# Moving each triangular inversion next to the chain that uses it, in a delta-rule and two-layer MoE kernel

## The chip, the cores and the metric

The kernel runs on one core of a Trainium2 chip. The metric is the device time of one execution in microseconds. Three runs of the kernel before took 5598.62, 1131.16 and 1135.46 us, so the median is 1135.46. The engines are named as the profile names them: PE does matmuls (PEld loads their weights), DVE, ACT and POOL do elementwise work, SP issues DMAs.

## The reference

Three stages follow each other: a delta-rule attention over 768 steps for 4 batches of 8 heads of 48 features, and two feed-forward layers of 384 to 2048 to 384 on the 3072 resulting tokens.

```
k_n = k / (norm(k) + 1e-6)
for t in range(S):                                   # state: D x D for each batch and head
    y[t]  = q[t] @ state
    v_old = k_n[t] @ state
    state = state + beta[t] * outer(k_n[t], v[t] - v_old)
x = y as 3072 tokens of 384
h = x @ w_in1;  g = where(h > 0, h, exp(min(h, 0)) - 1);  x = g @ w_out1
h = x @ w_in2;  P = a0 + a1 h + a2 h^2 + a3 h^3;  Q = 1 + |b0||h| + |b1| h^2
out = (P / (Q + 1e-6)) @ w_out2
```

All of it is float32. The kernel takes the weights as raw 64-bit words and converts them itself.

## The kernel before, in words

**Windows.** The 768 steps are cut into 12 chunks of 64 steps. Two chunks (512 tokens of the feed-forward layers) make a window; there are six, 0 to 5. While the first layer works on the tokens of window w, the attention of window w + 1 is computed beside it. Before window 0 lies a startup, and after window 5 the second layer (phase 2).

**What a window of the first layer does.** It has 16 steps f. Each f has nine large matmuls H (lines 578 to 580, two parts of each operand, so three products), the activation A1 on ACT (lines 607 to 609), B1 on DVE (line 613), C1 (gh on ACT, line 619; gl on DVE, line 621), and nine large matmuls O (lines 596 to 598). PSUM has two places for H, and gh, gl, e and pe have two buffers each. At the start of a window `split_x` makes xh (ACT, line 396) and xl (DVE, line 397) from the attention's output; at its end `evac1` (line 634) moves the layer's output out, one third of it by way of the tile `tmp`.

**What the attention of a window needs.** First the g groups (`g_item`, eight a window): eight matmuls each (line 279) of loaded keys and queries, evacuated on DVE (line 282) and ACT (lines 286 to 288) into gd, p and lo. Then the inversion (`t_pieces`): a transposition of gd (line 297), a run of tiny DVE and ACT steps (lines 301 to 333, with a large product at 324), 23 pairs of a product (line 345, always into `tmp`) and a sum (line 346) which invert 32 triangular matrices a partition (seven pairs of 8 rows, eight of 16, then four large pairs into xx_t and four into the remaining corner of tt), and a last transposition into tp_t (line 372). The tiles am, tt, tmp and tp_t exist once. Then the chain, for each of the two chunks: prep (kv on POOL, line 422; lb on ACT; four tb on POOL, line 432, out of tp_t), ks (line 449) with R on DVE (line 452), u1 (line 460) with its copies on ACT (line 463), lo (line 471) with its subtraction on DVE (line 475), u2 (line 483) with ub on ACT, the outputs y (lines 498 and 505), xx, and ku with the update of the state s_bd (line 535).

**Conversions.** 128 halves of weight tiles are loaded as raw words, treated on ACT (lines 160 and 162), then on DVE (line 179 for the first layer's 64; 176 and 177 for the second's), on ACT (180) and POOL (182), and split on ACT (71) and POOL (72).

**What sets the order.** Every step is entered in a list with a number for its place (`at(t, fn)`; one f is 1, a window 16). The list is sorted by it, and between the first steps and phase 2 a scheduler takes the numbers as priorities: it puts each engine's instructions into a fixed order, in which an instruction that it thinks isn't ready yet is passed by others. On the chip each engine runs its own order strictly. In the kernel before, window w works on the inversion of window w + 2 (numbers T + 0.6 to T + 9, where T = 16 w) and, from T + 0.6 to T + 14, on the chain of window w + 1.

Of the kernel before, what the change touches and what calls it, by code (L numbers as in the profile page):

```python
# [19 lines left out]
NF = 16  # L20
# [6 lines left out]
HD = DM // 2  # L27
NV = 15
Q = dict(
    ma=-200, xo=2.244, pg0=0, pg1=2, ca=0, g1=-72.135, g1d=1.259, t1a=-33.632, t1b=-8, npre=3, c0=-47,  # L30
    c0d=4.533, c1=-1.042, c1r=4.439, b1=0.704, c1o=0.919, h0=1.013, h0d=0.5, h1=0.586, h1d=0.462, g2=-7.824,
    g2d=1.116, g3w1=-0.578, g3=-0.806, t2=2.578, t2b=14.166, t3b=9, p=14.315, tm=4, chd=1.061, ws=0.808,
    sx=-0.529, ev=16.5, c5=1.1, c5d=0.4, l5=1.3, wu0=0, wl0=2, wd0=5, wy0=2, wm0=2, wu1=6, wl1=7, wd1=6, wy1=0,
    wm1=6, wk=4, wr=3, wr0=4)
# [3 lines left out]
def kernel(  # L38
# [19 lines left out]
    NW = len(WINS)  # L58
# [209 lines left out]
    def g_item(j, s, b):  # L268
        u0 = 16 * j + 4 * b
        if b == 0:  # L270
            p_d[s] = ap2.tile([128, 16, 64], F32, tag="p", name="p", bufs=4)
            lo_d[s] = ap2.tile([128, 8, 32], F32, tag="lo", name="lo", bufs=4)
        p_t, lo_t = p_d[s], lo_d[s]
        v0 = 4 * b
        ps = pa.tile([128, 4, 128], F32, tag="pa", name="gp")
        for p2 in range(2):
            t, n = gin_t.pop((s, b, p2))
            for i in range(2):
                mm(out=ps[:, 2 * p2 + i], lhsT=t[:, i, 0:128], rhs=t[:, i, 128:256], start=True, stop=True)  # L279
            gin_l[0] -= n  # L280
            gin_ahead(1)
        nc.vector.tensor_tensor(
            out=p_t[:, v0:v0 + 4], in0=ps[:, :, 64:128],
            in1=mp_sb[b // 2].unsqueeze(1).to_broadcast([128, 4, 64]), op=ALU.mult)
        b0, b1 = halves(b // 2)
        act(out=gd[b0, u0:u0 + 4], in_=ps[b0, :, 0:32], func=AF.Copy)
        act(out=gd[b1, u0:u0 + 4], in_=ps[b1, :, 32:64], func=AF.Copy)
        act(out=lo_t[b0, v0 % 8:v0 % 8 + 4], in_=ps[b0, :, 32:64], func=AF.Copy)
# [270 lines left out]
    def g_list(w):  # L559
        return [(lambda j=j, s=s, b=b: g_item(j, s, b)) for j, s in enumerate(WINS[w]) for b in range(4)]  # L560
# [21 lines left out]
    def H(key, f, x, NC):  # L582
        i = hn[0] % (2 if h_c is None else 3)
        hn[0] += 1
        ps = h_c if i == 2 else h_a[:, i]
        hp[key, f] = ps
        h_mms(ps[:, 0:NC], f, x, NC)

    def O(key, f, hi, lo, NC):
        gh, gl = gt.pop((key, f))  # L590
        if f == 0:
            acc[key] = [po.tile([128, 512], F32, tag=f"o{i}", name=f"o{i}") for i in range(3)]
        for c in range(3):
            ps = acc[key][c]
            cs = slice(128 * c, 128 * c + 128)
            mm(out=ps[:, 0:NC], lhsT=hi[:, cs], rhs=gh[:, 0:NC], start=(f == 0), stop=False)  # L596
            mm(out=ps[:, 0:NC], lhsT=hi[:, cs], rhs=gl[:, 0:NC], start=False, stop=False)  # L597
            mm(out=ps[:, 0:NC], lhsT=lo[:, cs], rhs=gh[:, 0:NC], start=False, stop=(f == NF - 1))  # L598
# [157 lines left out]
    def at(t, fn, *a):  # L756
        ev.append((t, len(ev), fn, a))

    def spread(t0, t1, fns, cost=None):
        cost = cost or [1.0] * len(fns)  # L760
        c = 0.0
        for fn, d in zip(fns, cost):
            at(t0 + (t1 - t0) * c / sum(cost), fn)
            c += d
# [33 lines left out]
    def t_at(w, t0, t1, t2, t3):  # L798
        tp = t_pieces(w)
        at(t0, tp[0])  # L800
        at(t0 + .3, tp[1])
        el = [4 * k * k for k in range(1, 8)] + [16 * k for k in range(8, 16)] + [1024, 768, 512, 256] + [256, 512, 768, 1024]
        spread(t1, t2, tp[2:-1], [.4 + .0021 * n for n in el])
        at(t3, tp[-1])

    def conv_at(t, d):
        at(t, conv_x)
        at(t + d, conv_d)
        at(t + 2 * d, conv_s)
# [9 lines left out]
    at(-55, load_beta, 1)  # L819
    for sl, fn in chain(0, [[0, 0, 1, 3, 5, 7, 10, 8, 11, 9], SLOTS[1]]):  # L820
        at(-48 + Q["chd"] * sl, fn)
    t_at(1, max(-47.5, Q["g1"] + 7 * Q["g1d"] + .01), Q["t1a"], Q["t1b"], Q["t1b"] + .1)
    for i in range(2 * Q["npre"]):
        conv_at(Q["c0"] + Q["c0d"] * i, 2)
    for i in range(4 * NF - 2 * Q["npre"]):
        conv_at(Q["c1"] + i / Q["c1r"], .24)

    for w in range(NW):
        T = 16 * w
        NC = 256 * len(WINS[w])  # L830
        at(T + Q["sx"], split_x, w)
        for f in range(NF):
            at(T + f, lambda w=w, f=f, NC=NC: H(w, f, xt[w], NC))
            at(T + f + .05, A1, w, f, NC)
            at(T + f + Q["b1"], B1, w, f, NC)
            at(T + f + Q["c1o"], C1, w, f, NC)
            at(T + f + Q["ws"], wo_split, w, f)

            def o1(w=w, f=f, NC=NC):
                t = oring.pop((w, f))  # L840
                O(w, f, t[:, 0], t[:, 1], NC)
            at(T + (f + 2.4 if f < NF - 2 else f + 1.95 if f == NF - 2 else f + 1.4), o1)
        at(T + Q["ev"], evac1, w)
        if w + 1 < NW:
            c0, cd = (Q["h0"], Q["h0d"]) if w == 0 else (Q["h1"], Q["h1d"])
            for sl, fn in chain(w + 1):
                at(T + c0 + cd * sl, fn)
        if w + 2 < NW:
            at(T - .2, load_beta, w + 2)
            for i, fn in enumerate(g_list(w + 2)):  # L850
                at(T + (Q["g2"] + Q["g2d"] * i if i < 4 else (Q["g3w1"] if w == 1 else Q["g3"]) * (8 - i)), fn)
            if w == 0:
                t_at(2, Q["t2"], Q["t2"] + .5, Q["t2b"], Q["t2b"] + .1)
            else:
                t_at(w + 2, T + .6, T + 1.2, T + Q["t3b"], T + Q["t3b"] + .1)
        if 1 <= w <= 4:
            for f in range(8):
                conv_at(T + 2 * f + .15, .5)

    T = 16 * (NW - 1)  # L860
# [12 lines left out]
    for k in range(NP * NG2):  # L873
        t = P + 2 * k
        at(t, H2, k)
        if k == NK - 1:
            for i in range(2):
                n = slice(512 * i, 512 * i + 512)
# [117 lines left out]
```

## Time and profile before

| | us |
|---|---|
| median of three runs | 1135.46 |
| the profiled execution | 1129.3 |
| its span | 1127.5 |
| PE busy | 1037.9 |
| DVE busy | 904.5 |
| ACT busy | 771.7 |
| POOL busy | 466.4 |

The span begins with the first instruction and ends with the last. Busy time of PE counts overlapping matmuls once and contains their pipeline, so a PE that is busy isn't at its peak; the granted clock (PEclk, 1.00 is 2.4 GHz, 0.50 is 1.2 GHz) has to be read beside it. A stretch of the run is read by the busy time of each engine in it, and the waits and the chain of waits tell which engine the others stood behind. B1 (line 613) runs once for each f, so its starts show how fast the loop goes.

### The profile page before, as it was taken

The page shows a single profiled execution, that of the slowest core. Times are in us where ns is not written, and L with a number is a line of the kernel's source. Part 1 is how long each engine was busy: PE and PEld are TensorE (multiplying, and loading weights), DVE is VectorE, ACT ScalarE, POOL GpSimd, SP SyncE. Part 2 cuts the span into 40 slices and gives each one's busy share as a digit, 9 for nine tenths or more (in the row PEclk, how much of TensorE's full clock was granted, in tenths as well). Part 3 has the DMA queues.
Part 4 walks back from the last instruction along what each step waited for, and adds up shares of the span by engine and source line. Part 5 has one row for each costly group of instructions (what it writes and reads, how often), then busy time and mean ns, then how long its engine had stood idle before and what let it go on. Part 6 is the DMA issues. An engine that isn't in the chain of part 4 may idle for free.

```text
span 1127.5 us, 20636 instructions
## 1 busy us (share of the span) xinstructions
PE 1037.9 (92%) x7952; PEld 835.8 (74%) x7952; DVE 904.5 (80%) x1240; ACT 771.7 (68%) x1525; POOL 466.4 (41%) x399
## 2 busy tenths in 40 slices
PE   7178898889798999899999999999999999999997
PEld 7155676667676778777888878778788888888885
DVE  4989889689857873795434379999999999999997
ACT  5568687866577546665665689976767667676764
POOL 1376655434332322242332145446363544536342
PEclk8559899999899989998999999999999999999999
DMA  9436343454364113120212044400100001010000
GB/s 287 155 102 200 116 147 114 131 161 126 97 189 149 59 50 121 60 81 1 81 49 62 1 148 133 120 28 1 56 1 25 32 1 56 1 56 1 29 1 28
DMA packets 51842, 91.75 MB, mean 81 GB/s; under 512 B 7072, under 2 KB 29728, under 8 KB 51744
## 3 DMA queue, kind: packets, MB, share of 16 engines
q1 hardware_dynamic: 51744, 90.43, 25.8%
q8 instruction: 62, 1.02, 0.4%
q14 instruction: 36, 0.29, 0.1%
HBM read 77.83 MB, written 12.58 MB: 80 GB/s over the span
## 4 chain that ended last, share of the span: by engine, by line
PE 54%; DVE 24%; ACT 7%; issue 6%; DMA 5%; POOL 3%; SPq 0%; ACTq 0%; DVEq 0%; POOLq 0%
PE o L733 13%; PE h_a L578 6%; PE h_a L579 6%; PE h_a L580 6%; DVE tmp L345 5%; PE o L596 3%; PE o L597 3%; PE o L598 3%; PE h_b L578 2%; PE h_b L579 2%; PE h_b L580 2%; DMA raw<-w_out 2%; DVE tt L346 2%; PE gp L279 2%; DVE wo L695 2%
## 5 line engine op out<-in xcount | busy, mean ns | idle before, releaser
L710 POOL TENSOR_TENSOR gl<-wo 128x1024 fp32r<-128x1024 f32 x47 | 147.3, 3134 | 202.4 <-DVE wo L709 174.2
L72 POOL TENSOR_TENSOR wor<-wo,wor 128x384 fp32r<-128x384 f32 x96 | 109.1, 1137 | 268.0 <-ACT wor L71 260.3
L578 PE MATMUL h_a<-xh,wi 128*128 128x512 f32 x417 | 173.9, 417 | 10.1 <-ACT pe L608 8.8
L579 PE MATMUL h_a<-xl,wi 128*128 128x512 f32 x417 | 168.9, 405 | 3.7 <-DVE xl L397 3.7
L580 PE MATMUL h_a<-xh,wi 128*128 128x512 f32 x417 | 167.8, 402 | 0.0
L733 PE MATMUL o<-gh,wo 128*128 128x512 f32 x564 | 135.9, 390 | 0.4 <-ACT ys L741 0.4
L613 DVE SCALAR_TENSOR_TENSOR e<-e,pe 128x512 f32<-128x512 f32 x96 | 70.8, 737 | 75.4 <-ACT e L609 75.1
L733 PEld LDWEIGHTS o<-gh,wo 128*128 128x128 f32 x564 | 105.2, 188 | 23.8 <-ACT ys L741 2.4
L596 PE MATMUL o<-gh,wor 128*128 128x512 f32 x288 | 115.8, 410 | 0.0
L597 PE MATMUL o<-gl,wor 128*128 128x512 f32 x288 | 114.5, 398 | 1.2 <-DVE gl L621 1.2
L598 PE MATMUL o<-gh,wor 128*128 128x512 f32 x288 | 113.0, 392 | 0.0
L578 PEld LDWEIGHTS h_a<-xh,wi 128*128 128x128 f32 x417 | 80.8, 194 | 30.5 <-ACT pe L608 10.9
L621 DVE TENSOR_TENSOR gl<-e,gh 128x512 fp32r<-128x512 f32 x88 | 79.2, 900 | 29.3 <-ACT gh L619 28.9
L579 PEld LDWEIGHTS h_a<-xl,wi 128*128 128x128 f32 x417 | 81.3, 195 | 22.1 <-DVE xl L397 7.2
L607 ACT ACTIVATE e<-h_a 128x512 f32<-128x512 f32 x91 | 54.2, 596 | 58.6 <-PE h_a L580 58.2
L580 PEld LDWEIGHTS h_a<-xh,wi 128*128 128x128 f32 x417 | 81.1, 194 | 17.3
L696 ACT ACTIVATE wo<-wo 128x1024 f32<-128x1024 f32 (+1 forms) x49 | 51.3, 1046 | 60.4 <-DVE wo L695 60.4
L619 ACT ACTIVATE gh<-e 128x512 fp32r<-128x512 f32 x96 | 60.0, 625 | 35.0 <-DVE e L613 35.0
L695 DVE SCALAR_TENSOR_TENSOR wo<-wo 128x1024 f32<-128x1024 f32 (+1 forms) x49 | 73.1, 1492 | 4.5 <-ACT wo L688 4.4
L71 ACT ACTIVATE wor<-wo 128x384 fp32r<-128x384 f32 x96 | 50.4, 525 | 35.7 <-PE o L598 35.3
L733 PE MATMUL o<-gl,wo 128*128 128x512 f32 x282 | 71.7, 389 | 0.8 <-POOL gl L710 0.8
L707 DVE SCALAR_TENSOR_TENSOR gh<-wo,ab_sb 128x1024 fp32r<-128x1024 f32 (+1 forms) x49 | 65.5, 1336 | 6.6 <-ACT wo L697 0.6
(168 smaller groups left out, 2462.8 us busy)
## 6 DMA issues: line engine op xcount, KB each, us to landing
kv<-c_kv SPq DMA_DIRECT2D x24, 576.0 KB, 4.6
gin<-g_in SPq DMA_DIRECT2D x69, 192.0 KB, 2.9
kq<-c_kq SPq DMA_DIRECT2D x22, 512.0 KB, 3.8
raw<-w_out SPq DMA_DIRECT2D x42, 192.0 KB, 2.5
raw<-w_in SPq DMA_DIRECT2D x34, 192.0 KB, 2.4
wo<-w_in SPq DMA_DIRECT2D x30, 192.0 KB, 2.7
xr<-x2d SPq DMA_DIRECT2D x6, 768.0 KB, 5.3
out_t<-ys SPq DMA_DIRECT2D x18, 256.0 KB, 2.2
```

Of the source, the lines that this page charges most:

```text
L72: eng.tensor_tensor(out=t[:, 1], in0=src, in1=t[:, 0].bitcast(F32), op=ALU.subtract)
L578: mm(out=ps, lhsT=hi, rhs=xh[:, c, 0:NC], start=(c == 0), stop=False)
L579: mm(out=ps, lhsT=hi, rhs=xl[:, c, 0:NC], start=False, stop=False)
L580: mm(out=ps, lhsT=lo, rhs=xh[:, c, 0:NC], start=False, stop=(c == 2))
L596: mm(out=ps[:, 0:NC], lhsT=hi[:, cs], rhs=gh[:, 0:NC], start=(f == 0), stop=False)
L597: mm(out=ps[:, 0:NC], lhsT=hi[:, cs], rhs=gl[:, 0:NC], start=False, stop=False)
L598: mm(out=ps[:, 0:NC], lhsT=lo[:, cs], rhs=gh[:, 0:NC], start=False, stop=(f == NF - 1))
L613: nc.vector.scalar_tensor_tensor(out=e, in0=e, scalar=-1.0, in1=p, op0=ALU.add, op1=ALU.add)
L621: eng.tensor_tensor(out=gl[:, 0:NC], in0=e, in1=gh[:, 0:NC].bitcast(F32), op=ALU.subtract)
L695: v.scalar_tensor_tensor(out=sq, in0=sq, scalar=1.0 + 1e-6, in1=ab, op0=ALU.add, op1=ALU.add)
L710: (v if k == NK - 1 else nc.gpsimd).tensor_tensor(out=gl, in0=sq, in1=ab, op=ALU.mult)
L733: mm(out=ps, lhsT=wo2[2 * j + i][:, int(p == 1), cs], rhs=(gl if p == 2 else gh)[:, n], start=(j == 0 and p == 0 and i == 0), stop=(j == N ...
```

## The change

Six inversions, their g groups and their chains are given other numbers; nothing is computed differently. From window 1 on, the g groups of window w + 1 stand at T - 11.6 to T - 6, its inversion at T - 5 to T + 4.1 (in window 0: -10 to 4.1), and its chain at T + 4.3 to T + 16. So the inversion for a chain now runs in the second half of the window before and the first quarter of the chain's own window, where before it ran one window earlier. The inversion of window 1 leaves the startup's numbers. 24 conversions instead of 6 have early numbers (-47 on, 1.9 apart instead of 4.533), and the others come 3.6 instead of 4.439 to one f.

```diff
-    ma=-200, xo=2.244, pg0=0, pg1=2, ca=0, g1=-72.135, g1d=1.259, t1a=-33.632, t1b=-8, npre=3, c0=-47,
-    c0d=4.533, c1=-1.042, c1r=4.439, b1=0.704, c1o=0.919, h0=1.013, h0d=0.5, h1=0.586, h1d=0.462, g2=-7.824,
+    ma=-200, xo=2.244, pg0=0, pg1=2, ca=0, g1=-72.135, g1d=1.259, t1a=-33.632, t1b=-8, npre=24, ta=-5, tb=4, hd=0.4, c0=-47,
+    c0d=1.9, c1=-1.042, c1r=3.6, b1=0.704, c1o=0.919, h0=1.013, h0d=0.5, h1=0.586, h1d=0.462, g2=-7.824,
...
-    t_at(1, max(-47.5, Q["g1"] + 7 * Q["g1d"] + .01), Q["t1a"], Q["t1b"], Q["t1b"] + .1)
-    for i in range(2 * Q["npre"]):
-        conv_at(Q["c0"] + Q["c0d"] * i, 2)
-    for i in range(4 * NF - 2 * Q["npre"]):
-        conv_at(Q["c1"] + i / Q["c1r"], .24)
+    for i in range(4 * NF):
+        n = Q["npre"]
+        conv_at(Q["c0"] + Q["c0d"] * i if i < n else Q["c1"] + (i - n) / Q["c1r"], 1 if i < n else .24)
...
         if w + 1 < NW:
-            c0, cd = (Q["h0"], Q["h0d"]) if w == 0 else (Q["h1"], Q["h1d"])
+            if w > 0:
+                at(T + Q["ta"] - 2, load_beta, w + 1)
+                for i, fn in enumerate(g_list(w + 1)):
+                    at(T + Q["ta"] - .2 + Q["g3"] * (8 - i), fn)
+            ta = Q["ta"] * (1 if w else 2)
+            t_at(w + 1, T + ta, T + ta + .6, T + Q["tb"], T + Q["tb"] + .1)
             for sl, fn in chain(w + 1):
-                at(T + c0 + cd * sl, fn)
-        if w + 2 < NW:
-            at(T - .2, load_beta, w + 2)
-            for i, fn in enumerate(g_list(w + 2)):
-                at(T + (Q["g2"] + Q["g2d"] * i if i < 4 else (Q["g3w1"] if w == 1 else Q["g3"]) * (8 - i)), fn)
-            if w == 0:
-                t_at(2, Q["t2"], Q["t2"] + .5, Q["t2b"], Q["t2b"] + .1)
-            else:
-                t_at(w + 2, T + .6, T + 1.2, T + Q["t3b"], T + Q["t3b"] + .1)
+                at(T + Q["tb"] + .3 + Q["hd"] * sl, fn)
```

What becomes of it in the engines' orders is shown at three places.

On DVE, where window 3 begins, before the change: xl is the split of the new window's input, L297 to L324 the start of window 5's inversion.

```order
L613 SCALAR_TENSOR_TENSOR e<-e,pe 128x512
L297 STREAM_TRANSPOSE am<-gd 128x1024
L397 TENSOR_TENSOR xl<-xs,xh 128x512 x3
L621 TENSOR_TENSOR gl<-e,gh 128x512
L301 TENSOR_SCALAR x<-am 128x32
...
L323 TENSOR_SCALAR nb<-x 128x32
L331 STREAM_TRANSPOSE bt<-x 128x32
L324 TENSOR_TENSOR am<-am,nb 128x1024
L613 SCALAR_TENSOR_TENSOR e<-e,pe 128x512
```

And the same place in the change:

```order
L613 SCALAR_TENSOR_TENSOR e<-e,pe 128x512
L535 TENSOR_TENSOR s_bd<-s_bd,ku 48x8x48 x2
L621 TENSOR_TENSOR gl<-e,gh 128x512
L535 TENSOR_TENSOR s_bd<-s_bd,ku 48x8x48 x2
L613 SCALAR_TENSOR_TENSOR e<-e,pe 128x512
L397 TENSOR_TENSOR xl<-xs,xh 128x512 x3
L621 TENSOR_TENSOR gl<-e,gh 128x512
L613 SCALAR_TENSOR_TENSOR e<-e,pe 128x512
```

The start of an inversion has left this place, and the chain's last updates of the state (L535) have come up to it.

On DVE at f = 10 to 11 of window 2 no inversion was under way before the change; in the change the start of the one for window 4 stands there, between two B1, with one of the chain's R (L452) in its midst:

```order
L318 TENSOR_SCALAR t_4653<-t_4653 128x32
L319 RECIPROCAL rr<-t_4653 128x32
L452 TENSOR_TENSOR R<-kv,ks 128x384
L320 TENSOR_TENSOR x<-rr 128x32
...
L324 TENSOR_TENSOR am<-am,nb 128x1024
L333 TENSOR_SCALAR bm<-bt,mh_sb 128x32 x2
L345 TENSOR_TENSOR tmp<-tt,am 128x4
L346 TENSOR_REDUCE tt<-tmp 128x4
...
L613 SCALAR_TENSOR_TENSOR e<-e,pe 128x512
```

17 of the 23 pairs follow from here to f = 14, and the last six stand at f = 2 to 5 of the next window.

On PE in window 2, at the first chunk of window 3's chain, before the change: ks and u1 (L460) stand next to each other, ahead of H.

```order
L580 MATMUL h_a<-xh,wi_628 128x512
L449 MATMUL ks<-s_bd,kq 32x48 x64
L460 MATMUL cb<-R,tb 64x48 x16
L578 MATMUL h_a<-xh,wi_792 128x512
L579 MATMUL h_a<-xl,wi_792 128x512
```

And in the change, of which the nine H and the nine O are cut to their ends:

```order
L449 MATMUL ks<-s_bd,kq 32x48 x64
L578 MATMUL h_a<-xh,wi_941 128x512
...
L580 MATMUL h_a<-xh,wi_941 128x512
L279 MATMUL gp<-gin 128x128 x4
L596 MATMUL o_3889<-gh,wor 128x512
...
L598 MATMUL o_3891<-gh,wor 128x512
L460 MATMUL cb<-R,tb 64x48 x16
```

Now 18 large matmuls and a g group stand between ks and u1.

## Rows read from the trace of the kernel before

**Rows 1.** Stretches: length, busy us of engines (count), granted clock, DMA share, GB/s.

```profile
0.00:117.30 117.30, 75.23 (x750) 56.98 (x751) 94.17 (x198) 73.32 (x237) 57.11 (x80) 0.74 0.60 183
117.30:244.50 127.20, 113.51 (x1119) 90.32 (x1119) 104.95 (x194) 96.81 (x264) 64.40 (x78) 0.96 0.45 135
244.50:363.50 119.00, 106.17 (x1076) 84.25 (x1075) 91.89 (x174) 80.09 (x198) 42.38 (x39) 0.96 0.46 136
363.50:472.20 108.70, 103.13 (x1070) 83.55 (x1070) 72.57 (x125) 64.85 (x140) 30.07 (x31) 0.95 0.24 77
472.20:567.10 94.90, 90.93 (x996) 73.47 (x996) 63.15 (x102) 56.17 (x111) 31.64 (x28) 0.96 0.17 54
567.10:655.10 88.00, 87.76 (x942) 71.15 (x941) 34.51 (x48) 56.05 (x111) 22.96 (x22) 1.00 0.11 36
...
737.00:1127.50 390.50, 382.72 (x1679) 313.59 (x1677) 370.68 (x291) 265.72 (x272) 178.84 (x79) 1.00 0.07 22
```

**Rows 2.** Chain of waits, phase 2: start, us, what.

```profile
814.02 4.08 PE o L733 x18
```

**Rows 3.** Chain of waits, where window 3 begins.

```profile
461.20 0.69 DVE e L613
461.90 1.91 DVE am L297
...
463.83 3.52 DVE xl L397 x3
...
472.17 0.70 DVE e L613
...
475.81 0.47 DVE R L452
```

**Rows 4.** Timeline of DVE into window 4: start, us, instruction.

```profile
560.95 0.69 DVE L613 SCALAR_TENSOR_TENSOR e<-e,pe 128x512 f32<-128x512 f32 x1 [1.45 <-ACT e L609]
...
567.07 0.69 DVE L613 SCALAR_TENSOR_TENSOR e<-e,pe 128x512 f32<-128x512 f32 x1 [2.20 <-ACT e L609]
```

**Rows 5.** Waits of PE in windows 2 and 3: us in total, times, longest.

```profile
PE cb L460 <- DVE R L452: 8.1, 8, 2.4
```

**Rows 6.** Stretches: the two halves of window 1.

```profile
244.50:299.80 55.30, 49.03 (x661) 39.00 (x659) 54.30 (x99) 33.09 (x76) 22.26 (x19) 0.97 0.35 105
299.80:363.50 63.70, 57.14 (x416) 45.25 (x417) 37.59 (x77) 47.00 (x122) 20.12 (x20) 0.95 0.55 163
```

**Rows 7.** Groups of instructions: busy us, mean ns of one, idle before.

```profile
L345 DVE TENSOR_TENSOR tmp<-tt,am 128x144 f32<-128x144 f32 (+17 forms) x114 | 57.5, 504 | 2.1
...
L346 DVE TENSOR_REDUCE tt<-tmp 128x4 f32<-128x4 f32 (+18 forms) x114 | 45.9, 403 | 2.6
...
L345 DVE TENSOR_TENSOR tmp<-xx_t,tt 128x256 f32<-128x256 f32 (+3 forms) x24 | 35.2, 1465 | 0.3
...
L346 DVE TENSOR_REDUCE xx_t<-tmp 128x64 f32<-128x1024 f32 (+3 forms) x24 | 19.5, 814 | 0.4
```

**Rows 8.** Stretch of the startup, line 179 alone.

```profile
0.00:117.30 117.30, 16.79 (x34) 0.74 0.60 183
```

**Rows 9.** Chain of waits in the startup.

```profile
62.74 3.58 POOL tb L432 x4
...
82.65 4.37 DMA wo<-w_in
```

**Rows 10.** Stretch of window 2, line 279 alone.

```profile
363.50:472.20 108.70, 9.25 (x64) 9.00 (x64) 0.95 0.24 77
```

**Rows 11.** Stretches of four f: windows 2 and 3.

```profile
413.80:441.00 27.20, 27.20 (x248) 22.72 (x247) 8.49 (x15) 18.94 (x44) 7.09 (x8) 0.88 0.20 64
519.50:544.30 24.80, 24.65 (x226) 19.95 (x225) 7.43 (x12) 15.72 (x32) 7.66 (x8) 0.86 0.07 22
```

**Rows 12.** Timeline of the startup, DVE and POOL.

```profile
56.56 1.96 DVE L345 TENSOR_TENSOR tmp<-xx_t,tt 128x1024 f32<-128x1024 f32 x1
...
56.79 2.18 POOL L72 TENSOR_TENSOR wi<-ce,wi 128x192 fp32r<-128x192 f32 x1 [0.47 <-ACT wi L71]
```

## The prediction, made before the changed kernel ran

> **What bounds the kernel now.** The sum is made against the profiled execution: 1129.3 us, of which 1127.5 are the span. I read the stretches first [rows 1], cut where the first B1 of each window starts (B1 is the DVE's one step per f, line 613, so its starts are a clock of the loop). The reader is to see three things there. From 737 us on PE is busy 382.72 of 390.50 at a granted clock of 1.00, in pieces of 18 matmuls that take 4.08 us [rows 2], 0.227 us each; nothing of the change is there. Window 5 (655 to 737) has neither chain nor inversion, and the change leaves it alone. So it acts on the first 655 us: a startup of 117.3 us and windows 0 to 4 of 127.2, 119.0, 108.7, 94.9 and 88.0 us, together 537.8.
>
> The windows differ by what runs beside the same 288 large matmuls (288 x 0.227 = 65.3 us). Window 4 has a chain, no inversion, no g groups, no conversions: PE is busy 87.76 of 88.00 at clock 1.00, so 88 is the price of a quiet window. Window 3 adds one inversion (DVE 63.15 us, not 34.51) and costs 7 more. Window 2 adds the eight g groups too: 108.7. Window 1 adds 27 conversions: 119.0. The clock tells of stalls: 0.95 or 0.96 in windows 0 to 3, so a tenth of the time was at the lower level and some 5% of a window, 4 to 5 us, was lost to it.
>
> Second I read the chain of waits where a window begins [rows 3]: between two B1 (461.20 and 472.17, 11.0 us) it holds DVE almost alone: the inversion's transposition, 1.91, xl, 3.52, then a row of tiny steps up to L324. Into window 4, where no inversion starts, the same two B1 are 6.1 us apart [rows 4]. So the start of an inversion costs 4.9 us at a boundary. Third, the waits in windows 2 and 3: u1 (L460) waits 8.1 us for R of the DVE [rows 5], 4 a window, because ks and u1 stand next to each other on PE there. Last, window 1 by halves [rows 6]: in the first, DVE is busy 54.30 of 55.30 us: inversion and conversions share it, and DVE decides; in the second it is busy 37.59 of 63.70.
>
> **The change part by part.** Counted in the orders, nothing is added or removed; it is moved. In startup there are 40 instead of 45 of the product-and-sum pairs of L345/L346, in window 0 23 instead of 24, in windows 1 to 3 23 as before, in window 4 six instead of none. So the load of a window hardly changes; the place in the window does: an inversion starts at f = 10, runs 17 pairs beside the second chunk of the chain before, and does its last six pairs and the final transposition in f = 2 to 5 of the next window, right ahead of the chain that needs them.
>
> *Startup.* Five pairs leave, four of them large. A large sum takes 0.814 [rows 7], its product about as much: 4 x 1.63 and a small pair of some 0.8 are 7.3 us. Four more conversions come in (38 ahead of the first B1, 34 before) at 16.79 / 34 = 0.49 us of DVE each [rows 8]: 2.0. DVE is relieved of 5 us. It was busy 94.17 of 117.30 us, but the first chain also hangs on POOL (tb, 3.58) and a load of 4.37 [rows 9]. I take -4; bounds -7 (the conversions hidden) and +2 (no gain, and the four conversions delay a step).
>
> *Window 0.* Its g groups fall from 14 to 8, and one transposition at either end of an inversion leaves. What a g group costs is bounded by two rows: eight are busy 9.25 us, overlapped by others [rows 10], and four f with four of them took 27.20 us against 24.80 without, at nearly one clock [rows 11], so 4.8 for eight. I take 7 for eight, near the middle, hence up to 5 for six. No engine alone bounds this window (PE busy 113.51, DVE 104.95, ACT 96.81 of 127.20), and the large pairs that startup loses now run in it. -3; bounds -10, +5.
>
> *Window 1.* 17 pairs and the start of the inversion move from the half that DVE fills into the half where it has 26 us free. The pairs of an inversion are (57.5 + 35.2 + 45.9 + 19.5) / 6 = 26.4 us [rows 7], with two transpositions of 1.9 some 30. The last six pairs, four products of 35.2 / 24 = 1.47 with sums of 0.814 and two smaller pairs of about 1 each, are with the last transposition 13 of that. The first half keeps the 13 us and is then PE's: half a quiet window, 44, and half the g groups, 4, are 48, and 55.30 - 48 = 7. -7; bounds -12 (the boundary's 4.9 besides) and 0 (the second half grows by as much).
>
> *Window 2.* The boundary's 4.9 us goes. The 4 us of waits for R go too: now 18 large matmuls, 4.08 us, stand between ks and u1, against two R of DVE at 0.5 [rows 3]. What comes in its place I bound from the same rows. At f = 10 to 11 the transposition (1.91), what stood between xl and B1 at the boundary (467.35 to 472.17, 4.8 [rows 3]) and both R stand between two B1: 8 us of DVE where PE has one f and ks, 5, so the B1 is 3 late, and on ACT the copies of u1's result (L463) stand behind gh of that f (L619), which waits for this B1; lo on PE waits for the copies. I take 1.5 (nothing, if two buffers cover it; 4, if they cover none). At f = 2 to 5 DVE has 13 us of inversion and four f of B1 and gl, 0.7 each, 18.6 in all, where PE has 16.3: the last transposition comes some 3 us late, and u1 of the first chunk stands behind it by way of tb on POOL. I take 3; bounds 0 and 5. -4.9 - 4 + 4.5 = -4.4, rounded to -4; bounds -9 and +5. For the clock I change nothing: stalls go and stalls come.
>
> *Window 3.* It gets eight g groups it didn't have, in a window where PE is busy 90.93 of 94.90: +7. R's waits -4, the two new waits +4.5. +8; bounds +1, +15.
>
> *Window 4.* The last six pairs fall on a DVE that is busy 34.51 of 88.00, so they cost nothing themselves; but u1 waits for their end: +3; bounds 0, +8 (with the clock's 4).
>
> *Queues.* With an inversion go one load of beta and POOL's memsets of tt, with a g group its two loads on SP; window 3 gets sixteen of them. The DMA engines are busy 0.17 of the time there, POOL 31.64 of 94.90 us [rows 1]; I count them at nothing. Loads that collide would show as g waiting for gin, on PE.
>
> Sum: -4 - 3 - 7 - 4 + 8 + 3 = -7, so 1122 for a profiled execution. The two ordinary runs shown (1131.16 and the median, 1135.46) lie 2 and 6 above the profiled one; with 4 for that, **1126 us**. A measurement of this kernel can tell about 2%, 23 us, from no change, so this is a gain on paper that most likely reads as no change.
>
> **A rule to weigh.** A product of the inversion ran on DVE from 56.56 to 58.52; a split of a conversion on POOL started at 56.79 and took 2.18: it ended 0.45 after DVE let go [rows 12]. The Trainium skill, SBUF — State Buffer, "Who interferes with whom", says that a DVE instruction with two inputs in SBUF and a GpSimd instruction that reads SBUF shut each other out for the whole instruction, by order of issue. By that, the trace agrees. In the sum a conversion on POOL costs DVE nothing; what it costs if it comes first is the fourth rival.
>
> **The rivals.** *The inversion ends too late for its chain* (slower than before). Place: the last transposition, then tb, then u1, with every large matmul queued behind u1 on PE. For it: DVE has no room at f = 2 to 5 by my own count, and tt, am and tmp exist once. Against it: the four tb take only 3.58 us, and PE has an f, ks and g groups to do meanwhile. It decides from 2 us a window in windows 1 to 4: 4 x 2 = 8 eats the gain. With 5 more in each (one f of DVE late, and the clock's loss), -7 + 20 = +13: 1129 + 13 + 4 = 1146. Chance 0.18.
>
> *The stalls go and none comes* (faster by over 2%). If both new waits are covered, windows 2 and 3 cost 88 + 7 + 2, window 4 stays 88, window 1 104, window 0 119, startup -7: 505 against 537.8 is -33, with startup -40: 1093. For it: the DVE loads are spread, and PE has chunk or g work wherever DVE has pairs. Against it: the start of an inversion is as serial at f = 10 as at a boundary. Two thirds of the way, 1104, still counts. Chance 0.20.
>
> *The change does not do what it says.* Counts by window are the same but for six pairs and six g groups, and only four conversions move ahead of the first B1. If placing by readiness evens out the rest, the time is 1129 + 4 = 1133. Chance 0.08.
>
> *POOL first.* Four more conversions, two POOL instructions each, ahead of DVE's products beside the first chain. Priced by the split that was held up, 0.45 us once it ran [rows 12], they hold DVE for up to 8 x 0.45 = 3.6 us, which takes the startup's 4: 1130. Chance 0.08.
>
> **How the numbers follow.** The forecast has 0.46, the rivals 0.18, 0.20, 0.08 and 0.08. Faster by over 2% (below 1112): most of the second rival and a tail of the forecast, 0.23. Slower by over 2% (above 1158): the end of the first rival and a little beyond it, 0.09. The rest, 0.68, is within 2%. The range goes from two thirds of the way to the second rival to a little above the first: 1105 to 1150. Within it the forecast's own cases take 1114 to 1138.
>
> **What would show it.** Window 3 longer by about 8 and window 4 by about 3, windows 1 and 2 shorter: right, step by step. B1 to B1 at the start of windows 2 and 3 near 6 us, not 11. The wait of u1 for R gone from the list, one of u1 for tb or of lo for L463 in it. The first B1 near 113. I am wrong if window 3 isn't longer (g is cheaper than I took it), if u1's waits reach 5 us in windows 1 to 4, or if the startup hasn't moved: then the first chain never hung on DVE.

## The result and the profile after

The changed kernel takes **1123.61 us** (median of six runs, 1122.40 to 1126.08), beside 1135.38 for the kernel before: a ratio of 0.9911, 95% interval 0.9883 to 0.9939. Timed again on another occasion it took 1121.45 beside 1137.35, 0.9866 (0.9811 to 0.9920). So it is faster by 1%, less than the 2% that were called a difference. Its profiled execution took 1126.08 us (span 1124.2), the longest of its six; a second profile of it, from the second occasion, has a span of 1119.8.

Stretches of the changed kernel, cut as those of before [rows 1] where each window's first B1 starts: start and end, length, busy us (count) of PE, PEld, DVE, ACT and POOL, granted clock, DMA share, GB/s.

```profile
0.00:124.20 124.20, 84.11 (x871) 61.24 (x872) 88.77 (x188) 73.08 (x234) 58.27 (x84) 0.68 0.56 172
124.20:235.70 111.50, 100.25 (x928) 77.07 (x927) 90.80 (x178) 91.87 (x247) 54.79 (x67) 0.97 0.45 135
235.70:347.10 111.40, 103.04 (x1072) 82.62 (x1071) 82.68 (x161) 77.45 (x189) 40.13 (x38) 0.95 0.45 137
347.10:452.40 105.30, 100.59 (x1071) 81.49 (x1070) 71.16 (x124) 64.59 (x141) 29.70 (x30) 0.97 0.25 81
452.40:557.40 105.00, 100.75 (x1069) 81.44 (x1068) 72.05 (x123) 64.47 (x141) 29.50 (x30) 0.97 0.24 78
557.40:651.80 94.40, 89.45 (x942) 71.75 (x941) 47.84 (x61) 55.85 (x111) 28.86 (x26) 0.96 0.10 33
```

Beside the forecast, in us ("after" is the profile above, "after, again" the second profile of the same kernel, "best" the best variant found below):

| stretch | before | forecast | after | after, again | best |
|---|---|---|---|---|---|
| startup | 117.3 | -4 | 124.2 (+6.9) | 117.8 (+0.5) | 118.8 |
| window 0 | 127.2 | -3 | 111.5 (-15.7) | 111.8 | 114.3 |
| window 1 | 119.0 | -7 | 111.4 (-7.6) | 112.0 | 110.2 |
| window 2 | 108.7 | -4 | 105.3 (-3.4) | 104.5 | 100.1 |
| window 3 | 94.9 | +8 | 105.0 (+10.1) | 107.1 | 100.2 |
| window 4 | 88.0 | +3 | 94.4 (+6.4) | 95.1 | 89.6 |
| behind | 472.4 | 0 | 472.4 | 471.5 | 471.2 |

The boundary into window 3 in the changed kernel, timeline of DVE: start, us, instruction, idle time before it.

```profile
445.25 0.88 DVE L613 SCALAR_TENSOR_TENSOR e<-e,pe 128x512 f32<-128x512 f32 x1
446.05 1.88 DVE L397 TENSOR_TENSOR xl<-xs,xh 128x512 fp32r<-128x512 f32 x3
...
452.35 0.69 DVE L613 SCALAR_TENSOR_TENSOR e<-e,pe 128x512 f32<-128x512 f32 x1 [3.00 <-ACT e L609]
```

B1 to B1 it is 7.1 us, not 11.0 [rows 3]: the transposition and the tiny steps are gone from between them, and DVE is idle for 3.00. Window 1 by halves, cut at the B1 of f = 8 as in [rows 6]:

```profile
235.70:288.70 53.00, 48.09 (x493) 38.43 (x492) 36.20 (x57) 36.52 (x89) 20.72 (x21) 0.94 0.41 125
288.70:347.10 58.40, 54.95 (x581) 44.19 (x580) 46.48 (x105) 40.93 (x101) 19.41 (x17) 0.97 0.49 148
```

DVE's 54.30 and 37.59 have become 36.20 and 46.48: the work went where there was room. Yet the half that DVE filled is only 2.3 us shorter, and the other half 5.3. The g groups have moved as well. Their matmuls (line 279: length, busy us and count of PE and PEld) in the two halves, before and after:

```profile
244.50:299.80 55.30, 1.05 (x8) 1.05 (x8) 0.97 0.35 105
299.80:363.50 63.70, 9.03 (x56) 7.91 (x56) 0.95 0.55 163
```

```profile
235.70:288.70 53.00, 7.14 (x42) 6.21 (x43) 0.94 0.41 125
288.70:347.10 58.40, 3.88 (x24) 3.42 (x22) 0.97 0.49 148
```

So four of the seven groups of the second half are now in the first. That they took up there what DVE's relief gave is likely, but no run shows it by itself.

The waits of PE in windows 2 and 3 (in total, times, longest), where [rows 5] had 8.1 us for R:

```profile
PE cb L460 <- POOL tb L432: 6.6, 4, 2.0
PE cb L471 <- ACT R L463: 2.4, 4, 1.2
```

Both waits that the prediction named have come, and R's has gone. The larger one over windows 1 to 4, and in window 4 alone:

```profile
PE cb L460 <- POOL tb L432: 14.3, 8, 3.5
```

```profile
PE cb L460 <- POOL tb L432: 5.0, 2, 3.5
```

How it arises is seen at the start of window 2, in the timelines of DVE, POOL and PE:

```profile
365.74 1.21 DVE L346 TENSOR_REDUCE tt<-tmp 128x64 f32<-128x1024 f32 x1
366.86 0.68 DVE L613 SCALAR_TENSOR_TENSOR e<-e,pe 128x512 f32<-128x512 f32 x1
367.46 2.10 DVE L372 STREAM_TRANSPOSE tp_t<-tt 128x1024 f32<-128x1024 f32 x1
...
369.64 3.93 POOL L432 TENSOR_TENSOR tb<-tp_t,bm 128x256 f32<-128x256 f32 x4 [1.23 <-DVE tp_t L372]
...
369.58 0.39 PE L598 MATMUL o<-gh,wor 128*128 128x512 f32 x1
371.74 0.31 PE L460 MATMUL cb<-R,tb 64*64 64x48 f32 x2 [1.77 <-POOL tb L432]
373.62 1.09 PE L460 MATMUL cb<-R,tb 64*64 64x48 f32 x16 [1.58 <-POOL tb L432]
```

DVE ends the last transposition at 369.56; POOL needs 3.93 us for the four tb; PE has done its large matmuls at 369.97 and waits twice in u1, 1.77 and 1.58 us, with all later work queued behind it.

### The profile page after: what moved, and what is told of

Its sections match the earlier page's. It is cut to its first block, busy times and chain, and to the rows that moved or that the text cites. A ratio compares the mean times of both kernels' runs of the same rounds, so it can differ in the third digit from the quotient of the medians.

```text
span 1124.2 us, 20682 instructions
## 1 busy us (share of the span) xinstructions
PE 1039.3 (92%) x7952; PEld 831.9 (74%) x7952; DVE 896.4 (80%) x1240; ACT 772.1 (69%) x1525; POOL 459.2 (41%) x399
## 4 chain that ended last, share of the span: by engine, by line
PE 63%; DVE 15%; ACT 8%; issue 5%; DMA 4%; POOL 4%; SPq 0%; ACTq 0%; DVEq 0%; POOLq 0%
PE o L733 13%; PE h_a L578 6%; PE h_a L579 6%; PE h_a L580 6%; PE o L596 4%; PE o L597 4%; PE o L598 4%; PE gp L279 3%; PE h_b L578 2%; PE h_b L579 2%; PE h_b L580 2%; DVE tmp L345 2%; DMA raw<-w_out 2%; DVE wo L695 2%; POOL tb L432 2%
## 5 line engine op out<-in xcount | busy, mean ns | idle before, releaser
L578 PE MATMUL h_a<-xh,wi 128*128 128x512 f32 x417 | 172.4, 414 | 3.8 <-ACT pe L608 3.0
L580 PE MATMUL h_a<-xh,wi 128*128 128x512 f32 x417 | 165.7, 397 | 0.0
L613 DVE SCALAR_TENSOR_TENSOR e<-e,pe 128x512 f32<-128x512 f32 x96 | 73.4, 764 | 53.9 <-ACT e L609 52.7
L621 DVE TENSOR_TENSOR gl<-e,gh 128x512 fp32r<-128x512 f32 x88 | 75.5, 858 | 34.2 <-ACT gh L619 33.8
L597 PEld LDWEIGHTS o<-gl,wor 128*128 128x128 f32 x288 | 55.0, 191 | 16.3 <-DVE gl L621 5.8
```

Of the source, the lines that this page charges most:

```text
L578: mm(out=ps, lhsT=hi, rhs=xh[:, c, 0:NC], start=(c == 0), stop=False)
L580: mm(out=ps, lhsT=lo, rhs=xh[:, c, 0:NC], start=False, stop=(c == 2))
L613: nc.vector.scalar_tensor_tensor(out=e, in0=e, scalar=-1.0, in1=p, op0=ALU.add, op1=ALU.add)
L621: eng.tensor_tensor(out=gl[:, 0:NC], in0=e, in1=gh[:, 0:NC].bitcast(F32), op=ALU.subtract)
```

## Experiments: u1 behind the last transposition

**tb3.** The inversion ends one f earlier, the chain stays.

```diff
-npre=24, ta=-5, tb=4,
+npre=24, ta=-5, tb=3,
-                at(T + Q["tb"] + .3 + Q["hd"] * sl, fn)
+                at(T + 4.3 + .4 * sl, fn)
```

> Edit: each inversion ends one f earlier (at f = 3, not 4, from the same start), the chain stays where it is. Theory C (end of the inversion): u1 of the first group waits for tb because the last transposition is late; the waits of u1 for tb (6.6 us in windows 2 and 3 together) shrink to under 2, windows 1 to 3 are 2 to 4 us shorter each, the whole 6 to 12 shorter (about 1114). Theory D (DVE is full): what DVE does one f earlier it takes from B1 of that f; the waits move to h_a or to lo, windows 1 to 3 change by less than 1.5 each, the whole by less than 4.

Measured 1112.37 us, 0.9787 of before (0.9727 to 0.9848). Windows 2, 3 and 4: 101.1, 100.3, 91.9; the waits for tb in windows 2 and 3 fell to 1.4 us. Theory C, though window 1, which it had 2 to 4 shorter, stayed (111.7), and window 0 got 4 longer (115.6).

**late.** The other way round: the chain moves, the inversions stay.

```diff
-                at(T + Q["tb"] + .3 + Q["hd"] * sl, fn)
+                at(T + 5.3 + .36 * sl, fn)
```

> Edit: the chain of each window starts one f later (5.3, not 4.3) with its steps 0.36 f apart instead of 0.40, so that it ends where it did; the inversions stay where they are. Theory C: the waits of u1 for tb shrink to under 2 us in windows 2 and 3 and nothing else changes: 6 to 12 us shorter (about 1114). Theory D: u1 still waits, since tb is late by more than one f (DVE and POOL in order), or the steps of the chain, now nearer to each other, wait for each other (lo for the copies of u1, u2 for lo) as much as was gained: the whole within 4 us of the changed kernel.

Measured 1109.32 us, 0.9766 (0.9717 to 0.9815). Stretches of windows 2 to 4 of this run:

```profile
346.10:446.20 100.10, 98.07 (x1073) 79.67 (x1072) 71.00 (x124) 64.55 (x141) 30.91 (x30) 1.00 0.26 86
446.20:545.60 99.40, 97.18 (x1069) 78.96 (x1068) 70.01 (x123) 64.34 (x141) 30.80 (x30) 1.00 0.26 82
545.60:636.10 90.50, 87.65 (x942) 69.91 (x941) 46.49 (x61) 55.94 (x112) 28.30 (x26) 1.00 0.10 35
```

No wait for tb is left in windows 2 and 3, and they are 5.2 and 5.6 us shorter than in the changed kernel. PE's idle time (length less busy time) fell by 2.7 and 2.0, since small new waits came in for those of u1 and lo that went; its busy time fell by 2.5 and 3.6 for the same matmuls. That second part goes with the clock, 1.00 now and 0.97 with the waits. Where it was lost is seen right behind the two waits of u1 in window 2 of the changed kernel (1.77 and 1.58 us, timeline above):

```profile
373.00:379.80 6.80, 6.18 (x44) 5.60 (x45) 1.30 (x2) 1.99 (x6) 2.56 (x4) 0.50 0.18 60
```

A stretch of 6.8 us at 1.2 GHz costs up to 3.4, and windows 3 and 4 have the same (from 478.8 and from 581.2 us). Windows 0 and 1 got 3.4 and 2.6 longer, so theory C's "nothing else changes" did not hold, and the whole gain, 14 us, is over its 6 to 12. The Trainium skill, TensorE: Matmul & The Clock Gate, "HAM oscillation — how this bites in real kernels", describes a kernel in which a wait of PE for a load brings the clock down, so that the work behind it starts at the lower one. The rows above agree in kind; the waits on that page are longer than those of window 2.

**late6.** Half an f more.

```diff
-                at(T + Q["tb"] + .3 + Q["hd"] * sl, fn)
+                at(T + 5.8 + .34 * sl, fn)
```

> Edit: the chain starts another half f later (5.8) with its steps 0.34 f apart. Theory C says that the wait for tb is gone already in the run late, so nothing more is to be had: windows 2 to 4 as there (100.1, 99.5, 90.5) plus 0 to 2 for steps that wait for each other; 1109 to 1115. If u1 was still late in windows 0 and 1 (u1 took 5.4 us of PE's time in window 1 there), these get 2 to 4 shorter: 1104 to 1108.

Measured **1105.50 us** (1104.49 to 1106.08), 0.9727 (0.9682 to 0.9772): the best version, 2.7% under the kernel before and 16 us under the changed kernel (1121.45) timed beside it. Windows 2 to 4 are as in late (100.1, 100.2, 89.6); window 1 is 3.8 shorter (110.2), window 0 0.6. The time is that of the second case, but its reason is not: u1 waits no less in window 1 than in late (late, then late6):

```profile
PE cb L460 <- DVE R L452: 2.7, 2, 2.2
```

```profile
PE cb L460 <- DVE R L452: 3.6, 3, 2.0
```

What is less there is the waits of g for its loads (3.4 to 1.8) and for ACT (1.6, gone) and of O for gl (2.1 to 0.5); why they are is open.

**late_tb35.** Half of each.

```diff
-npre=24, ta=-5, tb=4,
+npre=24, ta=-5, tb=3.5,
-                at(T + Q["tb"] + .3 + Q["hd"] * sl, fn)
+                at(T + 4.8 + .38 * sl, fn)
```

> Edit: half of each: the inversion ends at f = 3.5, the chain starts at 4.8 with its steps 0.38 f apart. Theory C: u1 has the same distance to the last transposition as in the run late, and the steps of the chain have more room: windows 2 and 3 at 99 to 101 as there, window 4 at 90, the whole 1108 to 1112. Theory D: the denser pairs bring half the waits of the run tb3 back: 1110 to 1114.

Measured 1114.41 us, 0.9810 (0.9762 to 0.9859); windows 2 to 4 103.3, 104.4, 93.9. Waits for tb are back (3.8 us in windows 2 to 4). Theory C missed; theory D's time is just above its range. Two half steps did not add up to one whole; the reason may be which instructions come to stand between the transposition and u1, but no run shows that.

**late_lastT.** The run late, and the last inversion done within window 3.

```diff
-            t_at(w + 1, T + ta, T + ta + .6, T + Q["tb"], T + Q["tb"] + .1)
+            tb = Q["tb"] if w < NW - 2 else -1
+            t_at(w + 1, T + ta, T + ta + .6, T + tb, T + tb + .1)
```

> Edit: the run late, and the last inversion ends a whole window third earlier, at f = -1 of window 4, so that window 4 has no pairs, as in the kernel before. Theory C: window 4 goes from 90.5 to 88, window 3 from 99.5 to 101 to 104 for six pairs more in f = 10 to 15: the whole 1108 to 1112, no gain. If pairs in window 3 are hidden (its DVE is busy some 72 of 99.5 us): 1106 to 1108.

Measured 1116.36 us, 0.9809 (0.9750 to 0.9868). Window 3 took 107.3, window 4 86.7. One wait heads window 3's list:

```profile
PE h_a L579 <- DVE xl L397: 4.4, 2, 2.4
```

Window 4 gave up its six pairs and 128 matmuls of a ks, 3.8 us, and window 3, which took them, is 7.8 longer, with DVE busy 82.84 us. Six pairs more in f = 10 to 15 are not hidden, although DVE is busy 70.01 of 99.40 us in that window of late: the share of a whole window says nothing of its last third. Theory C, above its range; part of that is the startup of this profile (123.0), and the runs spread from 1107.81 to 1118.38.

## Experiments: the price of the g groups

**gback.** The g groups of the window after next run at the end of the window before, so that window 3 has none.

```diff
-                for i, fn in enumerate(g_list(w + 1)):
-                    at(T + Q["ta"] - .2 + Q["g3"] * (8 - i), fn)
+            if w + 2 < NW:
+                for i, fn in enumerate(g_list(w + 2)):
+                    at(T - 4.7 + .6 * i, fn)
```

> Edit: the g groups of the window after next run at the end of the window before, as in the kernel before, so that window 3 has none (the inversion may then begin earlier, since gd is ready; it still ends at f = 4 of the window that uses it). Theory G (a g group costs what PE takes for it): window 3 is 7 to 9 us shorter than 105.0 (96 to 98), startup and window 0 together 7 to 9 longer, windows 1 and 2 within 2 of 111.4 and 105.3; the whole within 4 us of the changed kernel. Theory H (window 3 grew by the inversion's place, not by g): window 3 stays over 101.

Measured 1132.24 us, 0.9947 (0.9928 to 0.9966): 9 us over the changed kernel's 1123.61. Stretches of startup, windows 0, 1 and 3:

```profile
0.00:117.80 117.80, 76.00 (x751) 56.61 (x752) 87.29 (x188) 73.36 (x235) 56.03 (x82) 0.72 0.59 183
117.80:243.50 125.70, 108.64 (x1117) 87.09 (x1117) 95.57 (x188) 98.82 (x271) 59.49 (x69) 0.95 0.47 146
243.50:362.80 119.30, 103.32 (x1067) 82.47 (x1067) 87.61 (x162) 76.79 (x188) 40.78 (x38) 0.93 0.41 125
...
468.30:567.00 98.70, 92.55 (x1006) 73.47 (x1005) 70.94 (x116) 57.83 (x117) 30.01 (x30) 0.97 0.16 55
```

Window 3 is 6.3 shorter than in the changed kernel, PE's busy time there 8.2. The difference is a wait that was not there: with gd ready early, the next inversion begins near f = 2 again, in among the end of the one before and the start of the chain, and u1 waits for its tiny steps on DVE (window 3):

```profile
PE cb L460 <- DVE t L314: 4.6, 1, 4.6
```

So this run moves the groups and the start of the inversions together. Window 0 is 14.2 longer. Its matmuls of line 279, here and in the changed kernel:

```profile
117.80:243.50 125.70, 17.70 (x112) 15.77 (x112) 0.95 0.47 146
```

```profile
124.20:235.70 111.50, 9.27 (x56) 7.60 (x56) 0.97 0.45 135
```

These are seven groups more, and with them come the 128 matmuls of a ks, which stand ahead of the first B1 in the changed kernel and in window 0 here (count of PE 1117 to 928). Window 1, whose groups are as many, is 7.9 longer, and the 119.0 of the kernel before is back (119.3); but by halves it is 54.0 and 65.3, against 53.0 and 58.4, so it is again the second half that differs, not the one that DVE fills (50.05 of 54.00). Theory G came near in window 3 (98.7, where it had 96 to 98 and theory H over 101); it was too low for window 0, and for window 1 and the whole it was wrong.

**late_gback.** Both edits.

> Edit: the chain one f later with steps 0.36 f apart (as the run late) and the g groups a window earlier (as the run gback). Theory C (the place of u1 against tb is worth about 13 us, whatever else stands in the window) with G: 1109 plus or minus 4. If g and the inversion hold each other up in f = 10 to 15 (theory D), taking g away from there gives another 4 to 8: 1101 to 1105.

Measured 1121.56 us, 0.9847 (0.9819 to 0.9875): outside both ranges, 12 over late. Late's gain is there with the groups in their old place too (11 under gback). Window 3 is only 2.2 shorter than in late (97.3), and window 2, whose groups are as many, 4.5 longer (104.6): u1 waits 3.3 us for the tiny steps of the inversion in each. Theory D's gain did not come; since the inversions moved with the groups, whether the two hold each other up in f = 10 to 15 is not settled.

## Experiments: the startup

**after2.** The changed kernel again.

> No edit: the changed kernel once more, for a second profile of its startup, and timed beside the variants of the run late. Up to the first B1 its instructions stand in the same order on each engine as those of the run tb3, and on DVE as those of the run late; yet the first B1 came at 124.2 and 125.8 where the granted clock was 0.50 for 17.1 us from about 90 us on, and at 117.3 where it was so for 3.4 us. Theory A (the clock alone, which differs from execution to execution): the first B1 comes at 117 to 119 with under 7 us at the lower level, or at 123 to 126 with over 13, and the windows behind are as long as they were (111.5, 111.4, 105.3, 105.0, 94.4, each within 1.5). Theory E (the chain placed one f later relieves the startup): again 123 to 126 here, and 117 to 119 in all three variants of late. Whole: 1124 plus or minus 3.

Measured 1121.45 us, first B1 at 117.8. Theory A: nothing of the kernel differs, and the startup is 6.4 us shorter; only window 3 (107.1) is further from the first profile than the 1.5 that were allowed. Stretch 90 to 105 us of the first profile of the changed kernel, and of the second (the clock stands behind POOL's count):

```profile
90.00:105.00 15.00, 15.00 (x104) 8.48 (x103) 9.03 (x29) 8.51 (x27) 6.33 (x10) 0.50 0.37 108
```

```profile
90.00:105.00 15.00, 15.00 (x154) 8.18 (x155) 12.78 (x40) 12.32 (x40) 8.91 (x13) 0.87 0.50 151
```

PE was busy throughout in both, and did 104 matmuls in the one, at 1.2 GHz, and 154 in the other. The mean clock of 88 to 108 us against the first B1, over all profiles without added dummies: before 1.00 and 117.3; late 0.91, 117.3; late_tb35 0.91, 118.4; late_gback 0.91, 119.8; after2 0.85, 117.8; gback 0.83, 117.8; late6 0.83, 118.8; conv_old 0.83, 119.0; t1old 0.74, 121.7; late_lastT 0.74, 123.0; tb3 0.58, 125.8; after 0.57, 124.2. Roughly, the lower the clock, the later the first B1. And only the one profile of the kernel before has 1.00: in all eleven of changed versions the clock falls there, and what differs between the two executions of one program is for how long. In the changed kernel PE pauses just before it; its wait of u1 in the first and the second profile, from 84 us on, which the kernel before does not have:

```profile
PE cb L460 <- DVE R L452: 2.3, 2, 1.7
```

```profile
PE cb L460 <- DVE R L452: 1.9, 2, 1.6
```

**warm, warm2.** Dummy multiplications where PE paused. In warm between ks and u1 of the second group; in warm2 also behind u1. (Line numbers are 1 and 2 higher than in the changed kernel.)

```diff
-                    warm(kq[:, 0, 0:16], Q["wk"])
+                    for _ in range(3):
+                        warm(kq[:, 0, 0:16], 8)
```
```diff
-                        warm(d["tb"][:, 0, 0], Q[f"wu{j}"])
+                        for _ in range(1 + 2 * j):
+                            warm(d["tb"][:, 0, 0], 8 * j)
```

> Edit: in the first chain of the startup, PE multiplies three dummy tiles of 512 columns between ks and u1 of the second group, where the changed kernel has one of 256. Theory A (clock): the startup got 6.9 us longer because PE paused there (86.7 to 89.7 us), and its granted clock fell to 0.50 from 90 to 105 us. Then the clock stays at 1.00 from 90 to 105, u2's 16 matmuls take 1.1 us and not 1.9, the first B1 comes at 117 to 119 instead of 124.2, and the whole is 4 to 7 us shorter than the changed kernel (about 1118). Theory B (queues): the conversions that were put ahead delay the chain's own steps on POOL, DVE and ACT. Then the first B1 stays at 123 to 127, and the whole is the same or up to 3 longer.

> Edit: as the run warm (dummy multiplications between ks and u1), and behind u1 of the second group six dummy tiles of 512 columns instead of two of 384, since in the run warm PE paused 3.5 us there. Theory A (the clock decides the startup): with both pauses filled the granted clock is 1.00 from 90 to 105 us and the first B1 comes at 117 to 121, the whole 4 to 9 us under the run warm's 1128.7, in the profile and in the timed runs. Theory B (queues): the pause moves once more (lo to u2, or y), or the clock stays at 1.00 and the first B1 stays at 123 or later all the same: the whole 1126 to 1134.

Measured 1128.73 us (0.9948, 0.9915 to 0.9981) and 1133.07 (0.9956, 0.9937 to 0.9975), first B1 at 125.1 and 130.9. The pause moved, from R ahead of u1 to its copies ahead of lo, and then to R ahead of u2 (waits of PE from 84 us on, warm and warm2):

```profile
PE cb L472 <- ACT R L464: 3.4, 1, 3.4
```

```profile
PE cb L485 <- DVE R L477: 6.6, 1, 6.6
```

The clock fell to 0.50 at 93.9 us in warm, right behind that wait, and at 100.6 in warm2, within it. So theory A was right that the clock falls with a pause, and wrong of the cure; theory B's "the pause moves once more" came true. In warm the copies (L464) stood on ACT behind conversions, of which one (L180) waited 0.56 us for DVE's L179: the chain is held up by the queues of other engines, and PE kept busy with dummies got to the next such place.

**conv_old, t1old.** The conversions' numbers of the kernel before; the place of window 1's inversion of the kernel before.

```diff
-    for i in range(4 * NF):
-        n = Q["npre"]
-        conv_at(Q["c0"] + Q["c0d"] * i if i < n else Q["c1"] + (i - n) / Q["c1r"], 1 if i < n else .24)
+    for i in range(6):
+        conv_at(Q["c0"] + 4.533 * i, 2)
+    for i in range(4 * NF - 6):
+        conv_at(Q["c1"] + i / 4.439, .24)
```
```diff
-            t_at(w + 1, T + ta, T + ta + .6, T + Q["tb"], T + Q["tb"] + .1)
+            if w == 0:
+                t_at(1, max(-47.5, Q["g1"] + 7 * Q["g1d"] + .01), Q["t1a"], Q["t1b"], Q["t1b"] + .1)
+            else:
+                t_at(w + 1, T + ta, T + ta + .6, T + Q["tb"], T + Q["tb"] + .1)
```

> Edit: the weight conversions have the numbers of the kernel before (6 early ones 4.5 apart, the rest 4.4 per f, the order inside one as before), everything else as changed. Theory B (queues): the first B1 comes 5 to 8 us earlier (116 to 119), window 0 gets 2 to 4 longer, the whole 3 to 5 shorter. Theory A (clock): the place of the first B1 depends on whether PE pauses over 2 us between ks and u1 of the second group: with a pause the granted clock is 0.50 behind it and the first B1 stays at 122 to 126, without one it is 1.00 and the first B1 is near 118; either way the clock of the stretch 90 to 105 tells which.

> Edit: the inversion of window 1 has its place in the startup back (it ends ahead of f = 0), all others and the conversions as changed. Theory B (queues): 5 more pairs in the startup, 7 us of DVE: the first B1 2 to 7 later than with the changed kernel at the same granted clock (119 to 124 where the clock of 90 to 105 us is 1.00, 126 to 131 where it is 0.50), window 0 shorter by 1 to 4; the whole 0 to 5 longer. Theory A: the startup goes by the clock alone, near 118 or near 125, and window 0 gets up to 3 shorter: the whole -3 to +1.

Measured 1126.41 us (0.9920, 0.9890 to 0.9949) and 1130.70 (0.9940, 0.9903 to 0.9978). With the old conversions startup and window 0 are 119.0 and 111.3, near after2's 117.8 and 111.8, and PE pauses 2.0 us ahead of u1, as in the changed kernel. Theory B, which had window 0 longer and the whole 3 to 5 shorter, missed; so did theory A, which had the first B1 at 122 or later behind a pause of that length. That part of the change is worth nothing that can be told. With the old place of the inversion they are 121.7 and 115.4, 7.5 over after2's 229.6. Both theories had window 0 shorter, and it was longer; theory B's startup is within its wide ranges, and the whole, 7 over the changed kernel, is outside both. The runs spread from 1124.84 to 1133.59, so the size is not settled.

## Why the prediction held, and where it failed

**The total.** 1126 was forecast and 1123.61 measured. The sum of -7 against a profiled execution met -3.3 in the first profile and -7.7 in the second. It held in part by luck, by errors of opposite sign: window 0 gave 12 us more than forecast, startup and windows 3 and 4 together 13 to 16 less. The "+4 for ordinary runs" was a property of the one profile of before, not of the kernel: the changed kernel's first profile lies above its median.

**Startup (-4): failed.** The first B1 came no earlier than before, at its best 117.8 against 117.3. DVE's busy time fell from 94.17 to 88.77, by the 5 us worked out, but that too by luck: the pairs took 10.3 us with them, not 7.3 (L345 29.02 to 21.79, L346 20.43 to 17.35; the forecast took a large product at 0.81, where [rows 7] has 1.47), and the four conversions brought 4.7, not 2.0 (L179 16.79 to 21.50). The term that was missing is the clock. Behind the pause at u1 PE ran at 0.50 for 17.1 us in the first profile and for 6.8 in the second. At half the speed the difference makes up to 5.1 of the 6.4 us between the two, and the 6.8 lose up to 3.4, about what was to be gained (estimates from these rows). So the prediction's last sentence, that the first chain then never hung on DVE, is not shown: u1 there does wait for DVE's R. What decides how long PE stays at 1.2 GHz is open: two runs of one program differ. The Trainium skill, TensorE: Matmul & The Clock Gate, "What's actually happening", says that activity releases the throttle. Here PE was busy 15.00 of 15.00 us at 0.50, so busy time as the profile counts it did not.

**Window 0 (-3): mis-sized**, outside its bounds of -10 and +5. Eight groups were priced at 7 us, hence six at up to 5; seven of them left, and a ks with them. Gback gives 14.2 of the 15.7 back. How much of that is the groups' own price is open, as gback moves the start of an inversion too. Over startup and window 0 together, where the ks stays inside, eight groups make 13.9 between gback and the second profile of the changed kernel, and 8.7 between late_gback and late.

**Window 1 (-7): the number right, the place wrong.** The first half was to go from 55.3 to 48 and the second to stay; they went to 53.0 and from 63.7 to 58.4. The sum left out of the first half u1's wait for tb (2.8 in this window) and that more groups would run there. That the second half gave the rest is luck.

**Window 2 (-4): right**, also in its parts: 3.9 us at the boundary (4.9 forecast), R's wait gone, 1.4 for lo (1.5), 3.3 for u1 (3).

**Window 3 (+8): right in kind, too small.** Its waits and its clock went as forecast: 4.0 us of idle PE before and 4.3 after, at 0.96 and 0.97. What grew is PE's busy time, from 90.93 to 100.75, and the eight g groups alone (line 279; none before) are 9.95 of it, where 7 had been taken:

```profile
452.40:557.40 105.00, 9.95 (x64) 8.95 (x64) 0.97 0.24 78
```

**Window 4 (+3): right in kind, too small.** u1's wait is 5.0 us, not 3, and the clock fell from 1.00 to 0.96, by which PE's busy time grew by 1.7. Here, as in the startup, "for the clock I change nothing" was the error; in windows 2 and 3, where R's waits had cost clock before, it held.

**The rivals.** The first had the place right (last transposition, tb, u1) and its point of decision was passed, with 2.8, 3.3, 3.2 and 5.0 us in windows 1 to 4. By its own signs the prediction had called itself wrong at 5 us of these waits; they are 14.3 together. The price came on top of a gain in window 0 that was larger than forecast. It stood in the way of the second: with that wait gone (late6) the kernel is at 1105.5, near the second rival's two thirds. The third is out by the table. For the fourth, the conversions alone change nothing that can be told (conv_old).

## What to carry to other kernels

When a step is moved next to the one that uses it, leave room for the whole relay between them (here 6 us of transposition on DVE and four tb on POOL ahead of u1 on PE), and look for the queue that stands behind the waiting instruction: one f of distance more was worth about as much as the whole change. Count a stall of PE twice if the clock falls with it: in windows 2 and 3, taking the waits away gave 2.7 and 2.0 us of idle time back, and 2.5 and 3.6 of busy time besides. A piece of work has no one price: eight g groups cost 10 us of PE's time in window 3, and moving them drags along what was waiting for them.

## What the runs showed of the hardware

The same program, profiled twice, ran its startup in 124.2 and 117.8 us, with a granted clock of 0.50 and of 0.87 from 90 to 105 us, PE busy all the time in both. A wait of u1 of 1.77 and 1.58 us was followed by 6.8 us at 0.50; in the run late, where those for tb are gone or short, windows 2 to 4 ran at 1.00. With dummy multiplications meant to hold the clock up the startup took 125.1 and 130.9 us, no shorter than in either profile without.
